# Fourier layer between attention and feed-forward: token sums first, the folded columns of X as TensorE weights

## The chip, the cores and the metric

The kernel runs on one core of a Trainium2 chip. The metric is device time in microseconds (us) from the first to the last instruction of one execution. The kernel before took 1040.67 us (median of three runs, 1038.98 to 1045.13).

## What is computed

For each of 4 batches and 8 heads, queries, keys and values are 768 x 64. Queries and keys are assigned to one of 16 centroids by cosine; a score counts only where both have the same centroid. The attention output is laid out as X (768 tokens x 512 columns) per batch, goes through a two-dimensional Fourier transform of which only the real part is kept, and through a feed-forward layer with a residual:

```python
q_assign = np.argmax(np.einsum('bhsd,hcd->bhsc', q_n, c_n), axis=-1)
k_assign = np.argmax(np.einsum('bhsd,hcd->bhsc', k_n, c_n), axis=-1)
mask = q_assign[:, :, :, None] == k_assign[:, :, None, :]
scores = np.where(mask, scale * (q @ k.T), -1e9)
x = softmax(scores) @ v                      # as batch x 768 x 512
mixed = np.real(np.fft.fft(np.fft.fft(x, axis=1), axis=2))
u = x + mixed
un = (u - mu) / np.sqrt(var + 1e-06)         # over the 512 columns
out = u + np.maximum(un @ w_ch1, 0.0) @ w_ch2
```

All is float32 outside; inside, operands are split into two fp16 parts and three products are summed.

## The kernel before

**Attention** runs in steps. A head pair has six steps, one per block of 128 queries; four pairs make a batch, 16 pairs (96 steps) the whole. A step is written here as batch.pair.block. `scores` puts 12 matmuls L320 and 4 mask matmuls L325 on PE, then DVE L339 takes a maximum, ACT L342 the exponential and L350 its high half, POOL L351 the low half, and a DMA transpose L353 lays both out as `pt`. Two steps later (three in the first 22 steps) `attend` multiplies `pt` by V (L371 to L373, 36 matmuls); at blocks 2 and 5 of a pair `finish` (L383 to L387) divides and writes X. The preparation of the next pairs (`prep`: loads L206, maxima L216 and L248, scales L48, splits L235/L236, centroid choice L263 to L293) runs in the same steps.

**Fourier layer.** When all of X of a batch is there, `fold` adds and subtracts the two token halves and the two column halves (L641, L642: DVE and POOL), splits the result into fp16 parts (`halve`, ACT L625 and DVE L626) and has each part transposed by DMA (L648). `transform` first sums over columns: three chunks of the odd part and three of the even part (matmuls L697 with 257 moving columns, L712 for a middle row), with `rest` (six PE transposes L662 to L665) for one left-over column. Each result is split again (L625, L626). Then it sums over tokens in three thirds (L697, L746, L747); each third's result is added to and subtracted from X (ACT L758, DVE L759/L760, then L764 to L767 on DVE for third 0 and POOL for the others).

**Feed-forward** works in three blocks of 256 tokens. `norm` (L802 to L817) normalizes two of X's token tiles and has them transposed by DMA (L817); `up` is 16 chunks of 12 matmuls L846 with ReLU and split (L852 to L856); `down` is 8 chunks of 12 matmuls L877, each output tile finished by L881. The feed-forward chunks of batch b are the filler of the attention steps of batch b+1; the ones of batch 3 stand alone at the end.

**What sets the order.** `Overlap.run` writes the order of PE by hand, step by step; `MIX`, `KEEP` and a credit (`fill`) choose how many filler chunks stand between `scores` and `attend` of each step. DVE, ACT, POOL and SP follow a scheduler's priorities. All Fourier, feed-forward and preparation results on PE share a pool `ps_f` of three PSUM buffers; the temporary arrays of Fourier and feed-forward share one region of on-chip memory, `arena`. SP issues every DMA, in order.

## Time and profile before

| what | value |
|---|---|
| median of three runs | 1040.67 us |
| runs | 1038.98, 1040.67, 1045.13 us |
| profiled execution, its own span | 1037.9 us |
| mean granted TensorE clock | 0.949 |
| PE busy | 919.5 us (89%) |
| DVE, ACT, POOL busy | 594.6, 604.9, 587.9 us |
| first feed-forward matmul L846 of batch 0, 1, 2, 3 | at 260.05, 489.97, 715.05, 908.75 us |

The profiled execution stands 2.8 us below the median of the timed runs. A row of the timeline gives start, duration, engine, line, operation, output and inputs, count, and in brackets the engine's idle time before it and what ended it. A row of the windows view gives, after the window and its length, the busy time of each engine with the count of instructions, the mean granted TensorE clock, the mean busy share of the DMA engines and GB/s. A PE row's duration includes the drain of its last matmul, so the pace of matmuls is read from start to start.

### The profile page before, as it was taken

What the parts mean: (1) busy time and instruction counts of PE and PEld (TensorE: products, weight loads), DVE (VectorE), ACT (ScalarE), POOL (GpSimd) and SP (SyncE); (2) the same over time, 40 slices, a digit from 0 to 9 for tenths busy, and PEclk for the clock granted to TensorE, in tenths of its full rate; (3) what the DMA queues carried; (4) which work ended last, traced back from release to release, by engine and by line L of the source; (5) the groups of instructions that cost most, each with busy time, mean ns of one, the idle gap of its engine ahead of it and who ended that gap; (6) DMA issues with size and microseconds to landing.
All of it is one profiled execution on the core that took longest, in us unless ns stands there. A gap on an engine that the chain in (4) does not pass through costs nothing.

```text
span 1037.9 us, 23603 instructions
## 1 busy us (share of the span) xinstructions
PE 919.5 (89%) x9416; PEld 592.4 (57%) x9416; DVE 594.6 (57%) x1276; ACT 604.9 (58%) x948; POOL 587.9 (57%) x694
## 2 busy tenths in 40 slices
PE   4686777667999999997999999997999999899998
...
PEclk9688878889899999998999999998999999999999
...
GB/s 264 195 256 231 281 213 192 175 144 145 157 104 179 104 148 134 124 142 189 105 144 139 138 125 152 87 149 179 114 105 131 101 119 33 82 32 41 11 12 21
DMA packets 396239, 140.01 MB, mean 135 GB/s; under 512 B 381784, under 2 KB 381792, under 8 KB 396128
## 3 DMA queue, kind: packets, MB, share of 16 engines
...
## 4 chain that ended last, share of the span: by engine, by line
PE 47%; DVE 8%; POOL 7%; DMA 7%; ACT 6%; issue 5%; SPq 0%; ACTq 0%; POOLq 0%; DVEq 0%
PE ps_f L877 19%; PE ps_f L846 17%; PE ps_big L320 4%; DMA pt<-ph 4%; POOL ph L351 3%; DMA arena<-arena 3%; DVE ps_big L339 3%; ACT ph L350 2%; PE ps_o L371 1%; PE ps_o L372 1%; PE ps_o L373 1%; ACT p L342 1%; PE ps_big L325 1%; PE ps_f L697 1%; DVE arena L626 1%
## 5 line engine op out<-in xcount | busy, mean ns | idle before, releaser
L351 POOL TENSOR_TENSOR ph<-p,ph 128x768 f16<-128x768 f32 x144 | 242.0, 1690 | 179.9 <-ACT ph L350 152.5
L846 PE MATMUL ps_f<-arena,w1h 128*128 128x256 f16 x1536 | 272.1, 277 | 24.8 <-DMA arena<-arena 15.4
L877 PE MATMUL ps_f<-w2h,arena 128*128 128x512 f16 x768 | 238.9, 379 | 0.5 <-ACT arena L855 0.5
L846 PE MATMUL ps_f<-arena,w1l 128*128 128x256 f16 x768 | 212.5, 277 | 0.0
L342 ACT ACTIVATE p<-ps_big,rmx 128x768 f32<-128x768 f32 x144 | 129.1, 900 | 128.7 <-DVE ps_big L339 119.0
L877 PEld LDWEIGHTS <-arena 128*128 128x128 f16 x1152 | 108.7, 98 | 127.2 <-issue 5.8
L846 PEld LDWEIGHTS <-w1h 128*128 128x128 f16 x1536 | 152.3, 99 | 42.3 <-issue 21.0
L856 POOL TENSOR_TENSOR arena<-arena 128x256 f16<-128x256 f32 x192 | 128.2, 678 | 74.2 <-ACT arena L855 70.9
L339 DVE TENSOR_SCALAR_CACHE_REDUCE ps_big<-ps_big,sce 128x768 f32<-128x768 f32 x144 | 141.5, 1020 | 46.7 <-PE ps_big L325 46.7
L320 PE MATMUL ps_big<-hlk,hlq 64*128 64x384 f16 x1152 | 126.2, 344 | 30.3 <-ACT p L342 17.3
L877 PE MATMUL ps_f<-w2l,arena 128*128 128x512 f16 x384 | 145.5, 379 | 0.0
L371 PE MATMUL ps_o<-v,pt 128*128 128x66 f16 x1152 | 121.4, 196 | 12.4 <-DMA pt<-p 6.4
L855 ACT ACTIVATE arena<-ps_f,wrel 128x256 f16<-128x256 f32 x192 | 90.8, 475 | 70.5 <-DVE arena L852 68.7
L852 DVE TENSOR_SCALAR arena<-ps_f,wrel 128x256 f32<-128x256 f32 x96 | 46.3, 482 | 144.6 <-POOL arena L856 82.9
L350 ACT CAST ph<-p 128x768 f16<-128x768 f32 x144 | 117.3, 831 | 15.7 <-DMA pt<-ph 15.1
L371 PEld LDWEIGHTS <-pt 128*128 128x128 f16 x1152 | 108.5, 99 | 25.7 <-issue 13.5
L372 PE MATMUL ps_o<-v,pt 128*128 128x64 f16 x1152 | 121.1, 197 | 0.0
L373 PE MATMUL ps_o<-v,pt 128*128 128x66 f16 x1152 | 120.6, 195 | 0.0
L372 PEld LDWEIGHTS <-pt 128*128 128x128 f16 x1152 | 108.9, 99 | 2.8
L373 PEld LDWEIGHTS <-pt 128*128 128x128 f16 x1152 | 109.1, 101 | 0.0
L320 PEld LDWEIGHTS <-hlq 64*128 64x128 f16 x1152 | 54.6, 98 | 90.5 <-issue 60.0
L846 PEld LDWEIGHTS <-w1l 128*128 128x128 f16 x768 | 76.1, 99 | 20.0 <-issue 10.6
...
## 6 DMA issues: line engine op xcount, KB each, us to landing
...
```

The costliest lines, as they stand in the source:

```text
L320: nc.tensor.matmul(out=ps[j][:, hf, 0:SH], lhsT=hq[rows[j], a, sl], rhs=hk[rows[j], c, hs], start=(i == 0), stop=False)
L339: self.mark = nc.vector.tensor_scalar(out=ju, in0=ps[j][:, :, 0:SH], scalar1=ne, scalar2=None, op0=ALU.mult, op1=ALU.min, accum_out=m)
L342: nc.scalar.activation(x, ju, AF.Exp, bias=m, scale=-1.0)
L350: nc.scalar.copy(out=ph[:, 0], in_=p32)
L351: nc.gpsimd.tensor_tensor(out=ph[:, 1], in0=p32, in1=ph[:, 0], op=ALU.subtract)
L371: nc.tensor.matmul(out=o[:, at:at + W], lhsT=hi, rhs=v16[:, kt, 0:W], start=(kt == 0), stop=False)
L372: nc.tensor.matmul(out=o[:, at:at + D], lhsT=hi, rhs=v16[:, kt, 66:130], start=False, stop=False)
L373: nc.tensor.matmul(out=o[:, at:at + W], lhsT=lo, rhs=v16[:, kt, 0:W], start=False, stop=(kt == ST - 1))
L846: nc.tensor.matmul(out=ps.rearrange("p (t x) -> p t x", x=P), lhsT=a[:, dc, fs], rhs=c[:, :, dc], start=(i == 0), stop=(i == 11))
L855: nc.scalar.activation(hh[:, f], ps, AF.Relu, scale=rel[:, f:f + 1])
L856: nc.gpsimd.tensor_tensor(out=hl[:, f], in0=r, in1=hh[:, f], op=ALU.subtract)
L877: nc.tensor.matmul(out=ps, lhsT=a[:, f, ts], rhs=c[:, f], start=(i == 0), stop=(i == 47))
```

## The change

Token sums come first now, and need no transposes: a folded fp16 block of X with 128 tokens on the partitions and 128 columns is itself the weight of a matmul whose moving operand is a table row of 385 (cosine) or 384 (sine) frequencies. The output has columns on the partitions, and is the weight of the second sum (over columns, 257 moving columns).

- The fold is done in four units a, b, c, d (128 x 768 elements each). Units a and b (sine and cosine) use the columns of head pairs 0 and 3, c and d those of pairs 1 and 2. The head pairs of a batch are now taken in the order 0, 3, 1, 2 (`place`), so a and b can be folded when half of the batch's pairs are done.
- `tokens` A, B, C, D are the token sums of the four units: 9 matmuls L695 each, and two L715 for the middle token in B and D. `tokens256` (R) is the sum for column 256, as two rows: 7 matmuls L729/L731. `third` then sums over columns: 14 matmuls per third of tokens (L695, L764), and 8 more in third 0 for the middle frequency.
- The DMA transposes L648 (two per batch), the PE transposes of `rest`, and 119 matmuls per batch with 257 columns go; 47 matmuls with 384 or 385 columns and 50 with 257 come.
- The generator `layer` with `MIX` gives way to plans by step: relative to the step t of a batch's last attention, `a`, `b` and the tables at t-2, `A`, `B`, `c`, `d` at t-1, `C`, `D`, `R`, third 0 and `norm` at t, thirds 1 and 2 at t+1. An `o` in a plan is one feed-forward chunk of the batch before.
- The last block's `attend` of each batch is put one step earlier, and so is the end of the batch; `norm` of block 0 is issued after third 0 instead of after the matmuls of third 1; the tables come with one set of transfers; arena offsets move.

```diff
+def place(pr):
+    b, i = divmod(pr, H // 2)
+    return b, (0, 3, 1, 2)[i]
...
 class Fourier:
-    FOLDS = ((1, ALU.subtract), (0, ALU.add))
-    FE = (0, 0, 0, 1)
+    W = (SH + 1, SH)
+    UNITS = ((0, 1), (0, 0), (1, 1), (1, 0))
+    OPS = (ALU.add, ALU.subtract)
+    FE = ((0, 0), (0, 0), (0, 0), (0, 0))
...
+    def fold(self, b, u):
...
+        e0.tensor_tensor(out=f, in0=X4[:, 0:3, qs], in1=X4[:, 3:6, qs], op=op)
...
+        e1.tensor_tensor(out=f[:, :, 0, 1:P], in0=f[:, :, 0, 1:P], in1=f[:, :, 1, P - 1:0:-1], op=op)
+        h = at(self.FH[u % 2], [P, 2, 3, P], F16)
+        self.halve(f[:, :, 0], h[:, 0], h[:, 1], s)
...
+    def tokens(self, b, u):
...
+        ps = self.psf()
+        self.three(ps[:, 0:w], [((h[:, 0, k], h[:, 1, k]), (tab[0][:, k], tab[1][:, k])) for k in range(3)], last=bool(i))
...
+        with self.tc.high_priority():
+            self.split(ps[:, 0:w], y)
...
+    def columns(self, out, i, cols):
+        tab = (self.cd, self.sd)[i]
+        ys = [self.Y[c, i] for c in range(2)]
+        self.three(out, [((y[:, 0, cols], y[:, 1, cols]), (tab[:, 0, c], tab[:, 1, c])) for c, y in enumerate(ys)],
+                   last=bool(i))
...
-    COST, KEEP, KEEP3 = 130.4, 10.5, 7.9
+    COST = 124.8
...
-    MIX = (1, 0, 0, 0, 1, 0, 0, 1, 1, 0)
-    MIX3 = (0, 0, 0, 0, 0, 0, 0, 1, 1, 1)
-    F2 = 1
+    PLAN0 = ((-2, 3.6, "Sabg"), (-1, 1.5, "AB"), (-1, 3.6, "hcd"), (0, 1.5, "CD"), (0, 3.5, "R0n"), (1, 1.5, "12"))
+    PLAN = ((-2, 3.6, "Sabg"), (-1, 1.5, "oAB"), (-1, 3.6, "hcd"), (0, 1.5, "oCD"), (0, 3.5, "oR0n"), (1, 1.5, "o12oo"))
+    PLAN3 = ((-2, 3.6, "Sabg"), (-1, 1.5, "oAB"), (-1, 3.6, "hcdooCoDoR0no12oo"),)
+    F2, F1 = 2, -2
...
-                at(t0 + st + self.LAG + (6 * pr + st < self.LATE), 3, att.attend, pr, st)
+                at(t0 + st + self.LAG + (6 * pr + st < self.LATE) - (pr % 4 == 3 and st == 5), 3, att.attend, pr, st)
...
-        ends = [T0 + 24 * (b + 1) + self.LAG for b in range(B)]
+        ends = [T0 + 24 * (b + 1) + self.LAG - 1 for b in range(B)]
...
-            at(t, 0, self.fft.fold, b)
+            for dt, order, steps in self.PLAN if 0 < b < B - 1 else (self.PLAN3 if b else self.PLAN0):
+                at(t + dt, order, self.plan, b, steps)
```

Lines of the changed kernel are 6 or more higher than those of the kernel before: L320 is L326, L339 L345, L353 L359, L387 L393, L625/L626 are L629/L630, L802 to L817 are L826 to L841, L846 is L870, L877 L901.

**PE, batch 1, from third 0 to the first feed-forward matmul.** One row for each kind of work, in the order of its first appearance. Before:

```order
L697 MATMUL ps_f<-arena 128x257
...
L371 MATMUL ps_o<-v_5322,pt 128x66
...
L48 MATMUL ps_f<-ident,amx 128x128 x3
...
L320 MATMUL ps_big<-hlk,hlq 128x384
...
L877 MATMUL ps_f<-w2h,arena 128x512
...
L846 MATMUL ps_f<-arena,w1h 128x256
```

Changed:

```order
L764 MATMUL ps_f<-arena 1x257
...
L326 MATMUL ps_big<-hlk,hlq 128x384
...
L901 MATMUL ps_f<-w2h,arena 128x512
...
L695 MATMUL ps_f<-arena 128x257
...
L269 MATMUL ps_f<-hlq,ct 32x384
...
L377 MATMUL ps_o<-v_5367,pt 128x66
...
L870 MATMUL ps_f<-arena,w1h 128x256
```

Between third 0 and the first feed-forward matmul stood three attention steps (three `scores`, three `attend`), thirds 1 and 2, the scales L48 and two `down` chunks; now there stand two `scores`, one `attend`, thirds 1 and 2, the centroid matmuls L269 and two `down` chunks. The count of score matmuls L320 ahead of the first L846 of batches 0, 1, 2 goes from 384, 684, 972 to 336, 624, 912 (L326 ahead of L870): with 12 a step, the feed-forward layers begin 4, 5 and 5 attention steps earlier in the program. For batch 3 all 1152 stand ahead of it in both.

**DVE, batch 1, from the last write of X to the end of the fold** (X_64 is X of batch 1). Before:

```order
L387 TENSOR_TENSOR X_64<-ps_o,rs 128x3x128
L248 TENSOR_REDUCE amx<-vst 128x1
L852 TENSOR_SCALAR arena<-ps_f,wrel 128x256 x2
L339 TENSOR_SCALAR ps_big,rmx<-ps_big,sce 128x2x384 x2
L201 SCALAR_TENSOR_TENSOR v_6174<-vst,scp,v_6174 128x6x64
L641 TENSOR_TENSOR arena<-X_64 128x1536
L626 SCALAR_TENSOR_TENSOR arena<-arena,vseq 128x768
```

Changed:

```order
L393 TENSOR_TENSOR X_64<-ps_o,rs 128x3x128
L664 TENSOR_TENSOR arena<-X_64 128x768
L669 TENSOR_TENSOR arena<-arena 128x3
L670 TENSOR_TENSOR arena<-arena 128x3x127
L345 TENSOR_SCALAR ps_big,rmx<-ps_big,sce 128x2x384 x2
L630 SCALAR_TENSOR_TENSOR arena<-arena,vseq 1x129
L630 SCALAR_TENSOR_TENSOR arena<-arena,vseq 128x384
```

The fold of unit c follows the last write of X at once, with half the elements of the fold before; units a and b stand some steps ahead of these rows.

**DVE and SP, batch 1, from third 0 to the norm's transposes.** DVE before, between the first update of X and the statistics of the norm:

```order
L766 TENSOR_TENSOR X_64<-X_64,arena 128x257
L404 TENSOR_TENSOR ps_f<-ps_f,floor 128x3
L405 TENSOR_SCALAR ps_f<-ps_f 128x3
L407 TENSOR_SCALAR scp<-ps_f 128x3
L408 RECIPROCAL scp<-scp 128x3
L410 TENSOR_SCALAR sce<-scp 128x1 x2
L339 TENSOR_SCALAR ps_big,rmx<-ps_big,sce 128x2x384 x2
L802 BN_STATS bst<-X_64 128x6 x2
L236 SCALAR_TENSOR_TENSOR hlq<-scr,scp,hlq 128x768
L236 SCALAR_TENSOR_TENSOR hlk<-scr,scp,hlk 128x768
L803 BN_AGGR ps_f<-bst 128x2 x2
```

Changed:

```order
L789 COPY arena<-arena 1x257
L826 BN_STATS bst<-X_64 128x6
L790 COPY arena<-arena 1x257
L792 TENSOR_TENSOR X_64<-X_64,arena 128x255
L827 BN_AGGR ps_f<-bst 128x2
L791 TENSOR_TENSOR X_64<-X_64,arena 128x257
L345 TENSOR_SCALAR ps_big,rmx<-ps_big,sce 128x2x384
L826 BN_STATS bst<-X_64 128x6
```

SP, changed:

```order
L359 DMA_TRANSPOSE pt<-ph 128x12x128
L644 DMA arena<-in_cd_dram 128x1028
L644 DMA arena<-in_sd_dram 128x1028
L359 DMA_TRANSPOSE pt<-ph 128x12x128
L841 DMA_TRANSPOSE arena<-arena 128x8x128
L907 DMA out_dram<-arena 128x512
L841 DMA_TRANSPOSE arena<-arena 128x8x128
```

On DVE the scale and split work of the next head pair (L404 to L410, L236) no longer stands between the update and the statistics. On SP the two table transfers L644, which overwrite the tables that third 2 reads, stand ahead of one `pt` transpose and of the norm's two transposes L841.

274 lines of the change are left out of this document (136 added, 138 removed).

## The prediction

> **What bounds the kernel now.** I read the page first (shares, slices, chain), then the waits of PE, then windows and timeline around the four places where a batch passes from attention to feed-forward.
>
> ```profile
> span 1037.9 us, 23603 instructions
> ...
> PE 919.5 (89%) x9416; PEld 592.4 (57%) x9416; DVE 594.6 (57%) x1276; ACT 604.9 (58%) x948; POOL 587.9 (57%) x694
> ...
> PE   4686777667999999997999999997999999899998
> ...
> PEclk9688878889899999998999999998999999999999
> ```
>
> From slice 10 on (about 260 us) PE is at 9 or more in nearly every slice: it is the bound. The slices that dip are the passages of batches 1 and 2; those under 260 us are weight preparation, attention alone and the passage of batch 0. So past 260 us time changes by PE work added or removed and by PE's waits; before it, by when the first feed-forward matmul can start.
>
> The waits of PE (engine, line, what it waited for: us in all, times, longest):
>
> ```profile
> PE ps_big L320 <- ACT p L342: 17.3, 12, 3.5
> ...
> PE ps_f L846 <- DMA arena<-arena: 15.4, 4, 5.4
> ...
> PE ps_f L697 <- DMA arena<-arena: 3.9, 4, 1.3
> ...
> PE ps_f L271 <- DVE arena L626: 2.4, 1, 2.4
> ```
>
> The 15.4 us are the first L846 of each of the four batches, waiting for the norm's transposes. The windows of the passages:
>
> ```profile
> 189.80:270.50 80.70, 56.36 (x659) 38.01 (x658) 60.57 (x126) 47.23 (x73) 52.41 (x54) 0.83 0.80 164
> 439.80:452.10 12.30, 9.84 (x102) 5.97 (x103) 7.93 (x15) 6.08 (x10) 4.71 (x4) 1.00 0.48 111
> 474.90:500.60 25.70, 20.03 (x211) 13.47 (x212) 16.36 (x43) 16.71 (x29) 22.44 (x30) 0.87 0.83 180
> 663.50:675.60 12.10, 9.87 (x102) 5.99 (x103) 7.76 (x14) 6.09 (x10) 4.65 (x4) 1.00 0.47 109
> 698.40:725.70 27.30, 20.06 (x209) 13.58 (x208) 16.46 (x43) 16.71 (x29) 22.23 (x30) 0.81 0.82 165
> 880.00:910.00 30.00, 26.05 (x180) 15.46 (x178) 16.18 (x45) 8.72 (x18) 9.12 (x17) 1.00 0.40 88
> ```
>
> In the first, PE idles 80.70 - 56.36 = 24.3 us; around the fold of batches 1 and 2 12.30 - 9.84 = 2.5 and 12.10 - 9.87 = 2.2 us; around their first L846 25.70 - 20.03 = 5.7 and 27.30 - 20.06 = 7.2 us, with the clock down to 0.87 and 0.81; at the last passage 4.0 us. Work at the lower clock costs too: (1 - 0.87) x 25.7 = 3.3 and (1 - 0.81) x 27.3 = 5.2 us of clock, partly inside the waits. I put the loss of the three later passages at 11.5, 14.6 and 4.0 us at most (idle plus clock).
>
> How long the norm takes, from the first DVE operation on third 0 to the first L846, batches 0, 1, 2, 3:
>
> ```profile
> 205.43 0.56 DVE L387 TENSOR_TENSOR X<-ps_o,rs 128x384 f32<-128x384 f32 x1
> ...
> 237.53 0.48 DVE L759 SCALAR_TENSOR_TENSOR arena<-ps_f,vseq,arena 128x257 f32<-128x257 f32 x1 [1.86 <-ACT arena L758]
> ...
> 260.05 0.37 PE L846 MATMUL ps_f<-arena,w1h 128*128 128x256 f16 x1 [4.43 <-DMA arena<-arena]
> ...
> 464.43 0.49 DVE L759 SCALAR_TENSOR_TENSOR arena<-ps_f,vseq,arena 128x257 f32<-128x257 f32 x1 [0.57 <-ACT arena L758]
> ...
> 489.97 0.37 PE L846 MATMUL ps_f<-arena,w1h 128*128 128x256 f16 x1 [3.62 <-DMA arena<-arena]
> ...
> 687.92 0.48 DVE L759 SCALAR_TENSOR_TENSOR arena<-ps_f,vseq,arena 128x257 f32<-128x257 f32 x1 [0.57 <-ACT arena L758]
> ...
> 715.05 0.37 PE L846 MATMUL ps_f<-arena,w1h 128*128 128x256 f16 x1 [5.44 <-DMA arena<-arena]
> ...
> 893.11 0.49 DVE L759 SCALAR_TENSOR_TENSOR arena<-ps_f,vseq,arena 128x257 f32<-128x257 f32 x1 [1.78 <-PE ps_f L697]
> ...
> 908.75 0.27 PE L846 MATMUL ps_f<-arena,w1h 128*128 128x256 f16 x1 [1.92 <-DMA arena<-arena]
> ```
>
> That is 22.5, 25.5, 27.1 and 15.6 us. With no attention beside it the chain takes 15.6; attention's work on DVE and ACT adds 7 to 11.5.
>
> **The change part by part.** The sum is made against 1037.9 us, the profiled execution; the median of the runs stands 2.8 us above it.
>
> *PE work of the Fourier layer.* Gone per batch are 119 matmuls of 257 columns and 6 transposes; new are 47 of 384 or 385 columns and 50 of 257.
>
> ```profile
> 461.72 1.17 PE L697 MATMUL ps_f<-arena 128*128 128x257 f16 x9
> 462.82 0.28 PE L746 MATMUL ps_f<-arena 1*128 1x257 f16 x1
> ...
> 683.86 1.15 PE L320 MATMUL ps_big<-hlk,hlq 64*128 64x384 f16 x12
> 684.94 0.34 PE L325 MATMUL ps_big<-oht 32*128 32x384 bf16 x4
> ...
> 688.91 0.20 PE L371 MATMUL ps_o<-v,pt 128*128 128x66 f16 x1
> ...
> 690.02 0.91 PE L48 MATMUL ps_f<-ident,amx 128*128 128x128 f32 x6
> ...
> 883.81 0.82 PE L697 MATMUL ps_f<-arena 128*128 128x257 f16 x6 [1.14 <-DVE arena L626]
> 884.47 0.49 PE L662 MATMUL ps_f<-ident,arena 128*1 128x128 f32 x3
> ...
> 884.92 0.26 PE L665 MATMUL ps_f<-ident,arena 1*128 1x1 f32 x2
> 886.07 0.84 PE L697 MATMUL ps_f<-arena 128*128 128x257 f16 x6 [0.90 <-DMA arena<-arena]
> ...
> 929.91 20.72 PE ps_f L877 x96
> ```
>
> From start to start, 9 matmuls of 257 columns take 1.10 us, 0.122 each; 96 of 512 take 20.72, 0.216 each. In between, 385 columns come to 0.169 by interpolation. The nearest row with 384 columns is L320, two matmuls side by side: 6 pairs in 1.08 us, 0.180 a pair. The transposes keep PE from 884.47 to 885.18, 0.7 us. Before: 119 x 0.122 + 0.7 = 15.2; after: 47 x 0.169 + 50 x 0.122 = 14.0, or 14.6 with 0.180. I take -1.2 a batch; bounds -1.6 (0.162, in proportion to the 512-column row) and +1.0 (0.216, no cheaper than 512 columns). For batch 0 it lies among idle time, so three batches count: **-3.6** (-5 to +3).
>
> *Batch 0, the earlier start.* X is complete at 205.43 + 0.56 = 206.0 in both; before, the fold then needs until 237.53 to reach third 0's update. The new pieces, by the groups of DVE and ACT (count, busy, mean ns):
>
> ```profile
> L641 DVE TENSOR_TENSOR arena<-X 128x1536 f32<-128x1536 f32 x8 | 14.1, 1757 | 1.5 <-POOL arena L856 1.3
> L626 DVE SCALAR_TENSOR_TENSOR arena<-arena,vseq 128x768 f16<-128x768 f32 x8 | 9.2, 1154 | 19.3 <-ACT arena L625 19.3
> L642 DVE TENSOR_TENSOR arena<-arena 128x765 f32<-128x765 f32 x4 | 5.1, 1285 | 0.1
> ```
>
> A unit has half of each: 0.9 + 0.6 on DVE, some 0.5 on ACT, 0.6 on DVE, about 2.6 us; with the two maxima L339 of a step between, c is ready near 209 to 211 and d near 213 to 215. A and B have run by then. C, D, R and third 0 are 20 + 7 + 22 matmuls, about 7 us of PE, with a split of some 0.9 us behind D and behind R and a `scores` between: third 0's first DVE operation at 221 to 223, against 237.53. Add a norm chain of 19.5 to 22.5 (below) and the first feed-forward matmul comes near 243 in place of 260.05: **17 earlier**. But four attention steps that ran ahead of it now run behind it. A step's `scores` from 683.86 is 1.08 + 0.27 = 1.35 us, its `attend` (688.91 to 690.02) 1.1; with the preparation matmuls among them four steps are about 11.2 us of PE, which must be done later. About 1 us of new waits goes too. Gain 17 - 11.2 - 1 = **-5** (-16, if most of the moved work falls into time that is idle anyway, to +4, if the start is only 8 earlier).
>
> *Batches 1 and 2.* Gone: the waits on L648's transposes (3.9 us over four) and on splits, and the delay of the statistics by L404 to L410 and the two splits L236, which stood between L802 and L803:
>
> ```profile
> 474.39 1.00 DVE L236 SCALAR_TENSOR_TENSOR hlq<-scr,scp,hlq 128x768 f16<-128x768 f32 x1
> ```
>
> With its twin and the five small operations that is 3 to 4 us, and the statistics no longer wait for the updates of a later third. So the chain falls from 25.5 and 27.1 to about 20 (ends: 15.6, the chain without attention, and 27). Its cover shrinks too: between third 0 and the first feed-forward matmul PE had three `scores` and three `attend` (3 x 2.45), thirds 1 and 2 (36 + 4 matmuls, 4.8), two `down` chunks (2 x 2.59) and 0.9 of L48, about 18; it now has two `scores` (2.7), one `attend` (1.1), 28 matmuls of the thirds (3.4), 8 left of third 0 (0.9), the centroid matmuls (0.5) and two `down` chunks (5.2), about 14. The wait stays: 20 - 14 = 6, less what the last `scores` waits anyway, 5.2 to 5.7. PE also waits for c and d: d is ready some 5 us after the last `attend`, with 2.5 us of idle left, as in the fold windows before. With a split of R of 0.7, 1.7 for the clock (half of a stretch of 3.4 behind the wait) and 2.1 of small waits, as `scores` has them on L342, the passages cost 2.5 + 0.7 + 5.5 + 1.7 + 2.1 = 12.5 each, against 13.1 (11.5 and 1.6 of split waits) and 14.6: **-0.6** and **-1.9** (-8 to +7 each).
>
> SP: two table transfers L644 wait for third 2's last matmul ahead of the norm's transposes. Third 2 ends some 9 us behind third 0, the transposes are issued at 15 or later, so this hides; if PE lagged by 6 us it would not. DVE's four smaller folds replace about the same work; DVE is busy 57%.
>
> On the clock, the row at 489.97 shows a 3.62 us wait, and its window stands at 0.87, while 2.5 us of idle around the fold (439.80) left it at 1.00. The Trainium skill (TensorE: Matmul & The Clock Gate, "Part 1: The HAM clock gate") says that the clock halves after an idle window of about 3.4 us and needs a busy one to return, which agrees with these windows. By it the new 2.5 us wait for d would cost no clock, and only the one at the first feed-forward matmul would, as the sum has it; were those two waits to come out under that window, the sum would be 3.4 us lower.
>
> *Batch 3.* The fourth passage has only `down` chunks as cover. Its chain of 15.6 holds one wait on third 1:
>
> ```profile
> 898.71 0.42 DVE L803 BATCH_NORM_AGGREGATE ps_f<-bst 128x2 f32<-128x6 f32 x2 [1.60 <-ACT arena L758]
> ```
>
> Without it the chain is about 13.7. The cover had three `down` chunks and thirds 1 and 2; it now has two, those thirds and 8 matmuls, 5.2 + 3.4 + 1.0 = 9.6. So the wait of 1.92 grows to about 4; R's split adds 0.7, and the norm takes a third `ps_f` buffer earlier, which holds third 1 up by an update of X's 1.4 (L758, L759, L760, 0.48 each). The gone waits of 1.14 and 0.90 at the fold stand against it: **+2** (-2 to +7).
>
> Sum: -3.6 - 5 - 0.6 - 1.9 + 2 = -9.1; 1037.9 - 9.1 + 2.8 = **1031.6 us**.
>
> **Rivals.** *The norm does not get shorter* (slower). Attention's DVE and ACT work, which holds the chain at 25.5 and 27.1 against 15.6 alone, may hold it as before: the statistics are placed earlier, but DVE, ACT and POOL carry the same work in this passage (474.90: 16.4, 16.7 and 22.4 of 25.7). Then the cover of 14 leaves 11.5 and 13 us of waiting instead of 5.5: +6 and +7.5 on the -0.6 and -1.9 above. With the chain of 15.6 kept in the last passage that is +4; batch 0 gains 4 and the PE work 3.6. Sum 5.4 + 5.6 + 4 - 4 - 3.6 = +7.4: 1048. Each us of chain costs 2, so it decides from about 24 us on, where the 9.1 are used up. For it speaks that the parts on POOL (22.4 of 25.7 busy) do not move; against it that the two operations in front of the statistics do go.
>
> *The waits vanish.* If the chain comes to 15.6 in the middle passages too and less in the last, the three later waits (3.6 + 5.4 + 1.9 = 10.9) go, and of the 8.5 us of lower clock the 5 that I put outside them. With the PE work and batch 0 as above, 10.9 + 5 + 3.6 + 5 = 24.5: 1037.9 - 24.5 + 2.8 = 1016. The row at 893.11 speaks for it, DVE's load against.
>
> *Batch 0 does not gain.* The stretch up to 270 us has DMA at 0.80 and the clock at 0.83; weight, load and `pt` transfers may hold the earlier feed-forward back, and attention's steps behind it wait as before. Then the 5 fall away, or turn to +2: 1036 to 1039. That the change would simply do nothing is this case too: its PE work differs by 3.6 us alone.
>
> **Chances.** Forecast 0.48, no gain at batch 0 0.22, norm not shorter 0.17, waits vanish 0.13. A difference under 0.5% (5.2 us) can't be told from none. Faster by more needs under 1035.5: nearly all of the first and last, a little of the second: 0.6. Slower, over 1045.9: 0.2, with what of the forecast's bounds lies there. Within: 0.2. The forecast's own bounds reach 1018 to 1045; the range takes in both rivals' ends, 1012 to 1048.
>
> **What would show it.** The first L870 at about 243 (right if before 248, wrong if after 252). In batches 1 and 2, third 0's first DVE operation to the first L870 under 22 us, and a wait there of 5 to 6; over 24 the slower rival holds. A wait of 2 to 3 us ahead of D's matmuls. L695 with 385 columns 0.16 to 0.18 apart. The clock below 1 only behind the first L870. If batch 0 is early and the end is not, the moved attention steps were dearer than 11.2 us.

## The result

The changed kernel is slower: 1079.9 us median (1075.66 to 1084.92, 4 runs) against 1040.38 us (4 runs), a ratio of 1.037 (95% interval 1.032 to 1.043). The forecast was 1031.6 us. The profiled execution took 1073.8 us, 35.9 us more than the 1037.9 us of the one before; it was the fastest of the four, and the medians lie 39.5 us apart. All step times and losses below are read from one profiled execution of each kernel. The page of the changed kernel:

```profile
span 1073.8 us, 23394 instructions
...
PE 922.1 (86%) x9284; PEld 584.1 (54%) x9304; DVE 603.8 (56%) x1316; ACT 605.8 (56%) x952; POOL 586.4 (55%) x694
...
PE   4667675678997989889989989889989999989998
...
PEclk9798888788998999999999999899999999999999
```

PE, DVE, ACT and POOL are busy about as long as before. But from slice 10 on PE shows 8 in many slices that read 9 before, and these lie between the passages from attention to feed-forward, not only in them. The waits of PE (engine, line, what it waited for: us in all, times, longest):

```profile
PE ps_f L870 <- ACT arena L879: 28.1, 16, 5.5
PE ps_big L326 <- DVE X L345: 19.4, 20, 4.3
PE ps_f L870 <- DMA arena<-arena: 19.2, 4, 8.6
PE ps_f L695 <- ACT arena L629: 10.7, 4, 6.5
PE ps_big L326 <- ACT p L348: 7.7, 8, 2.0
```

The third row is the wait for the norm's transposes that the forecast dealt with (15.4 before). The first is new in size: feed-forward matmuls that wait for the ReLU and split on ACT, inside the attention steps. How long the norm takes, from third 0's first DVE operation to the first L870, batches 0 to 3:

```profile
227.12 0.49 DVE L784 SCALAR_TENSOR_TENSOR arena<-ps_f,vseq,arena 128x257 f32<-128x257 f32 x1 [1.21 <-PE ps_f L695]
...
246.94 0.37 PE L870 MATMUL ps_f<-arena,w1h 128*128 128x256 f16 x1 [8.62 <-DMA arena<-arena]
...
463.57 0.49 DVE L784 SCALAR_TENSOR_TENSOR arena<-ps_f,vseq,arena 128x257 f32<-128x257 f32 x1 [1.22 <-PE ps_f L695]
...
482.37 0.39 PE L870 MATMUL ps_f<-arena,w1h 128*128 128x256 f16 x1 [2.99 <-DMA arena<-arena]
...
703.94 0.49 DVE L784 SCALAR_TENSOR_TENSOR arena<-ps_f,vseq,arena 128x257 f32<-128x257 f32 x1 [1.22 <-PE ps_f L695]
...
722.94 0.27 PE L870 MATMUL ps_f<-arena,w1h 128*128 128x256 f16 x1 [3.19 <-DMA arena<-arena]
...
928.40 0.49 DVE L784 SCALAR_TENSOR_TENSOR arena<-ps_f,vseq,arena 128x257 f32<-128x257 f32 x1 [1.21 <-PE ps_f L695]
...
943.31 0.37 PE L870 MATMUL ps_f<-arena,w1h 128*128 128x256 f16 x1 [4.38 <-DMA arena<-arena]
```

19.8, 18.8, 19.0 and 14.9 us, against 22.5, 25.5, 27.1 and 15.6. So the passages did get what the forecast saw in them, and batch 0 starts 13 us earlier. The time went elsewhere. From here on a step is written as pair.block, with the 16 pairs counted from 0 to 15 over the whole kernel, and not as batch.pair.block: batch 0 has pairs 0 to 3, and step 4.0 is the first of batch 1. The stretches between the passages are steps 5.2 to 8.0, 9.5 to 12.0 and 13.5 to 15.4 ("mid-way" below); the feed-forward of batches 0, 1 and 2 is the filler there. Their windows, first of the kernel before, then of the changed one:

```profile
270.50:414.60 144.10, 139.61 (x1586) 93.41 (x1587) 82.54 (x175) 88.91 (x143) 92.95 (x106) 1.00 0.69 131
517.70:637.00 119.30, 118.23 (x1305) 77.48 (x1304) 68.54 (x147) 72.99 (x114) 74.72 (x84) 1.00 0.72 134
742.80:843.90 101.10, 100.19 (x1078) 62.95 (x1077) 47.26 (x104) 57.60 (x89) 60.07 (x65) 1.00 0.60 111
```

```profile
287.00:439.80 152.80, 142.08 (x1580) 92.28 (x1579) 91.89 (x189) 88.52 (x140) 91.91 (x101) 0.97 0.71 137
545.80:676.30 130.50, 119.49 (x1349) 81.13 (x1348) 78.28 (x158) 78.16 (x127) 81.44 (x90) 0.97 0.70 138
786.80:888.30 101.50, 91.42 (x1054) 61.52 (x1053) 51.83 (x110) 60.19 (x96) 63.80 (x67) 0.97 0.67 121
```

PE's idle time (length less PE busy) was 4.5 + 1.1 + 0.9 = 6.5 us; it is 10.7 + 11.0 + 10.1 = 31.8. And the clock, 1.00 before, is 0.97 in all three: 0.03 x 384.8 = 11.5 us. Together 25.3 + 11.5 = 36.8 us that the forecast did not have. In the changed kernel all of this idle time is in waits for ACT: 12 of the 16 waits of L870 for L879 lie in these windows, 24.1 of the 28.1 us, and the 8 waits of L326 for L348, 7.7 us.

For an account of the whole, each step's length less its matmuls at the pace of undisturbed steps (`scores` 1.35, `attend` 1.11, an `up` chunk 1.31, a `down` chunk 2.59, a 257-column matmul 0.122, a 385-column one 0.17, small preparation 0.45 to 0.55 each) gives what PE lost there by waits and clock, in us:

| steps | before | changed | difference |
|---|---|---|---|
| up to 3.5 (step 4.0 begins at 189.8, now 193.9) | 90.6 | 94.7 | +4.1 |
| 4.0 to 5.1, passage of batch 0 | 36.3 | 30.2 | -6.1 |
| 5.2 to 8.0 | 6.6 | 17.4 | +10.8 |
| 8.1 to 9.4, passage of batch 1 | 14.8 | 14.3 | -0.5 |
| 9.5 to 12.0 | 2.1 | 16.4 | +14.3 |
| 12.1 to 13.4, passage of batch 2 | 16.2 | 18.7 | +2.5 |
| 13.5 to 15.4 | 2.0 | 14.0 | +12.0 |
| 15.5 to the end | 4.8 | 8.1 | +3.3 |

(In the first row 20 matmuls whose records are missing from the trace of the changed kernel are counted as work.) The sum is +40.4 us, and the matmul work by these prices is 4.5 us less: +35.9, the difference of the spans. The three mid-way rows are 10.7 before and 47.8 now, +37.1. All losses below are counted in this way.

One of these stalls, step 6.0 of the changed kernel: PE, ACT and SP.

```profile
327.07 0.37 PE L870 MATMUL ps_f<-arena,w1h 128*128 128x256 f16 x1 [4.81 <-ACT arena L879]
```

```profile
325.45 0.83 ACT L356 CAST ph<-p 128x768 f16<-128x768 f32 x1 [5.36 <-DMA pt<-ph]
```

```profile
314.02 2.64 SPq L841 DMA_TRANSPOSE arena<-arena  x2
317.32 0.38 SPq L642 DMA_DIRECT2D arena<-in_ss_dram  x1
317.75 0.48 SPq L642 DMA_DIRECT2D arena<-in_cs_dram  x1
...
320.09 0.28 SPq L644 DMA_DIRECT2D arena<-in_ny_dram  x1
320.48 4.17 SPq L359 DMA_TRANSPOSE pt<-ph  x2
```

PE waits for a ReLU (L879) that stands on ACT behind L356; L356 waits 5.36 us for a buffer that the last `pt` transfer must first have read; that transfer stands on SP behind the second norm's transposes, token tables and `ny`. Steps 10.0 and 14.0 repeat it (waits of 4.85 and 5.53). These three steps lost 6.3, 6.4 and 7.0 us; the other 28 us lie in smaller waits at 6.1, 6.2, 7.1, 7.2, 7.4, 11.1, 11.2, 15.4 and others. (L879, one of the two ReLU operations of an `up` chunk, ran on ACT right behind this L356 and L878, at 326.55.)

**Theories.** *Thin filler*: the kernel before has the Fourier layer's matmuls and leftover feed-forward spread over steps 8.1 to 9.1; the change packs the Fourier layer and eight `down` chunks into steps 8.0 to 8.2, with 12.2, 19.0 and 11.6 us of matmul work there, and step 7.5 has 12.5. The other twenty steps of a batch then have less, and where a step's matmuls are shorter than what attention's DVE, ACT, POOL and DMA need for it, PE waits. *Queue*: tables and `ny` ahead of `pt` on SP. *Maxima*: the early loads put L222 ahead of L345 on DVE at 7.1 and 11.1. *ACT order*: ReLUs behind attention's casts. *Phase*: the feed-forward's start now falls elsewhere against the head pairs, so that `up` blocks meet the second norm at a bad place.

### The profile page after: what moved, and what is told of

Same layout as the page of the kernel before. It is cut to its first block, busy times and chain, and to the rows that moved or that the text cites. A ratio compares the mean times of both kernels' runs of the same rounds, so it can differ in the third digit from the quotient of the medians.

```text
span 1073.8 us, 23394 instructions
## 1 busy us (share of the span) xinstructions
PE 922.1 (86%) x9284; PEld 584.1 (54%) x9304; DVE 603.8 (56%) x1316; ACT 605.8 (56%) x952; POOL 586.4 (55%) x694
## 4 chain that ended last, share of the span: by engine, by line
PE 36%; DVE 16%; DMA 15%; POOL 12%; ACT 11%; issue 8%; SPq 1%; ACTq 0%; POOLq 0%; DVEq 0%
PE ps_f L870 16%; PE ps_f L901 10%; DMA pt<-ph 7%; POOL ph L357 5%; PE ps_big L326 3%; ACT ph L356 3%; DVE ps_big L345 3%; ACT p L348 2%; DMA scr<-in_q_dram 2%; DMA vst<-in_v_dram 2%; DVE X L345 2%; PE ps_f L695 2%; DMA scr<-in_k_dram 2%; POOL arena L880 2%; POOL arena L840 1%
## 5 line engine op out<-in xcount | busy, mean ns | idle before, releaser
L357 POOL TENSOR_TENSOR ph<-p,ph 128x768 f16<-128x768 f32 x144 | 237.1, 1655 | 214.8 <-ACT ph L356 196.7
L870 PE MATMUL ps_f<-arena,w1h 128*128 128x256 f16 x1536 | 274.6, 278 | 47.3 <-ACT arena L879 28.1
L901 PE MATMUL ps_f<-w2h,arena 128*128 128x512 f16 x768 | 242.4, 384 | 0.0
L870 PE MATMUL ps_f<-arena,w1l 128*128 128x256 f16 x768 | 213.2, 278 | 0.0
L348 ACT ACTIVATE p<-ps_big,rmx 128x768 f32<-128x768 f32 x144 | 129.4, 900 | 114.0 <-DVE ps_big L345 99.7
L901 PEld LDWEIGHTS <-arena 128*128 128x128 f16 x1152 | 109.7, 99 | 131.1 <-issue 12.5
L880 POOL TENSOR_TENSOR arena<-arena 128x256 f16<-128x256 f32 x192 | 134.8, 711 | 83.1 <-ACT arena L879 79.0
L870 PEld LDWEIGHTS <-w1h 128*128 128x128 f16 x1536 | 152.6, 99 | 45.8 <-issue 22.4
L345 DVE TENSOR_SCALAR_CACHE_REDUCE ps_big<-ps_big,sce 128x768 f32<-128x768 f32 x144 | 141.7, 1019 | 33.2 <-PE ps_big L331 33.1
L356 ACT CAST ph<-p 128x768 f16<-128x768 f32 x144 | 118.3, 834 | 61.8 <-DMA pt<-ph 61.5
L326 PE MATMUL ps_big<-hlk,hlq 64*128 64x384 f16 x1152 | 128.6, 348 | 28.4 <-DVE X L345 19.4
L901 PE MATMUL ps_f<-w2l,arena 128*128 128x512 f16 x384 | 147.5, 384 | 0.0
L377 PE MATMUL ps_o<-v,pt 128*128 128x66 f16 x1152 | 120.3, 196 | 13.1 <-DMA pt<-p 6.9
L879 ACT ACTIVATE arena<-ps_f,wrel 128x256 f16<-128x256 f32 x192 | 91.3, 476 | 61.2 <-DVE arena L876 60.8
L377 PEld LDWEIGHTS <-pt 128*128 128x128 f16 x1152 | 107.9, 98 | 26.5 <-issue 16.4
L326 PEld LDWEIGHTS <-hlq 64*128 64x128 f16 x1152 | 55.6, 99 | 88.8 <-issue 60.2
L870 PEld LDWEIGHTS <-w1l 128*128 128x128 f16 x768 | 76.3, 99 | 39.8 <-issue 30.5
```

The lines of the kernel that those rows point to most:

```text
L326: nc.tensor.matmul(out=ps[j][:, hf, 0:SH], lhsT=hq[rows[j], a, sl], rhs=hk[rows[j], c, hs], start=(i == 0), stop=False)
L345: self.mark = nc.vector.tensor_scalar(out=ju, in0=ps[j][:, :, 0:SH], scalar1=ne, scalar2=None, op0=ALU.mult, op1=ALU.min, accum_out=m)
L348: nc.scalar.activation(x, ju, AF.Exp, bias=m, scale=-1.0)
L356: nc.scalar.copy(out=ph[:, 0], in_=p32)
L357: nc.gpsimd.tensor_tensor(out=ph[:, 1], in0=p32, in1=ph[:, 0], op=ALU.subtract)
L377: nc.tensor.matmul(out=o[:, at:at + W], lhsT=hi, rhs=v16[:, kt, 0:W], start=(kt == 0), stop=False)
```

## The experiments

Ratios are to the kernel before, run beside each, with 95% intervals. The changed kernel stands at 1.037 (1.032 to 1.043). The intervals of e1, e2, e4, e6, e8 and e13 overlap with that, so there the losses of single steps say more than the time.

### The queue in front of the transposes

**e1_no_tables**

```diff
-        for nm in ("ss", "cs"):
+        if b:      # tables' names point at a weight tile
+            ...
+        for nm in ("ss", "cs") if not b else ():
```

> The changed kernel without the token tables' transfers (L642) in batches 1 to 3: there the token sums read a piece of the weights as if it were the table, so their result is not the reference's and only the time counts. Queue theory: in steps 6.0, 10.0 and 14.0 three table transfers stand on SP behind the norm's transposes and ahead of a step's pt transposes; pt is late, ACT's cast L356 waits for a free ph in order, the feed-forward's ReLUs wait behind it on ACT, and PE has no free PSUM buffer. Then the waits of 4.8, 4.9 and 5.5 us at 327, 564 and 806 us go with the slower clock behind them, 18 to 22 us in all: about 1059 to 1062 us. Thin-filler theory: the feed-forward of a batch is spread over 4 to 5 more attention steps, each has less to cover a late chain, and the transfers are only one of many small delays: at least 3 us of each wait stay, the time falls by less than 8 us, to 1072 or more.

1073.99 us, 1.033 (1.030 to 1.036). Step 6.0 still lost 4.5 (6.3), 10.0 2.9, 14.0 4.8; the three mid-way rows sum to 36.0 in place of 47.8. Tables have a part, a quarter of the mid-way loss (11.8 us); the time fell by 6 us and not by the 18 to 22 of the queue theory.

**e4_tables_later**

```diff
+    PLAN = ((-10, 3.6, "T"), ...       # T: three of the four table transfers,
+                with self.tc.issue_after(self.att.sent.ins):   # behind a pt transfer
+                    self.fft.ahead()
```

> The changed kernel with three of the four token-table transfers of batches 1 to 3 held on SP until the pt transposes of step x.3 of the batch's third pair are issued (6.3, 10.3, 14.3), so that they no longer stand between the norm's transposes and the pt of 6.0. Queue theory, place decides: as much is saved as without the transfers, 16 to 22 us, 1058 to 1064 us. If it is the transfers' load on the DMA engines and not their place in the queue, the wait moves to steps 6.4 or 6.5 and less than 8 us are saved. Thin-filler theory: less than 8 us too, with waits of 3 us or more left at 6.0, 10.0 and 14.0.

1073.85 us, 1.032 (1.028 to 1.035). That is 6 us less, under the 8 of the thin-filler line, and steps 6.4 and 6.5 did not lose more. Steps 6.0, 10.0, 14.0 lost 4.7, 4.2 and 4.6. What still stood on SP ahead of `pt` was `ny`, which waited 2.3 us for the norm's transposes to land.

**e16_queue_clear**

```diff
-        for nm in ("ny", "cm", "sd", "cd"):
+        for nm in ("ny", "cm", "sd", "cd")[bool(b):]:
...
+        self.nc.sync.dma_start(out=at(self.NY, [1, 2], F16), in_=self.con["ny"])   # in ahead()
```

> e4_tables_later, and the tiny transfer of ny (two numbers) is held back with the tables too. In e4_tables_later it was issued on SP only after the transposes of the second norm had landed (SP waited 2.3 us for it) with the two pt transfers of step 6.0 behind it; now nothing stands between those transposes and pt but one output transfer. Computation is complete. The losses of steps 6.0, 10.0 and 14.0 were 6.3, 6.4 and 7.0 us in the changed kernel, 4.7, 4.2 and 4.6 in e4_tables_later, 0.1 in the kernel before and in e15_before_thin. If the queue ahead of pt makes them: under 2.5 each, mid-way losses of 12, 12 and 11 in place of 14.6, 14.6 and 13.8, and 1073.9 - 7 = about 1067 (1063 to 1070). If the thin step itself makes them: 4 or more each, and 1071 to 1075.

1071.76 us, 1.026 (1.022 to 1.031). SP at step 6.0 of this kernel:

```profile
314.63 2.63 SPq L848 DMA_TRANSPOSE arena<-arena  x2
317.36 0.53 SPq L914 DMA_DIRECT2D out_dram<-arena  x1
318.70 4.23 SPq L359 DMA_TRANSPOSE pt<-ph  x2
```

`pt` is issued 1.4 us behind the transposes instead of 3.8, and steps 6.0, 10.0 and 14.0 lose 2.0, 2.0 and 2.5, about what the queue theory had (under 2.5): at these three steps the queue sets the wait (19.7 became 6.5). But the mid-way rows are 14.5, 14.4 and 10.6, not 12, 12 and 11, since other thin steps lose more: 6.2 3.3 in place of 1.9, 7.2 4.3 in place of 3.2, 11.2 4.4 in place of 3.1. Of 13.2 us taken away at the three steps, 8.3 were left in the mid-way sum. The time does not decide: the median, 1071.8, lies in the other theory's range, but the kernel before took 1045.12 beside this run, and the ratio of 1.026 makes about 1068 of the 1040.38 above, which is in the queue theory's range. By the steps each theory was half right: the queue says where the stall shows, not how much is lost.

### Maxima and ACT's order

**e2_pin_max**

```diff
-    PIN, PF, PV = (), 29, 1
+    PIN, PF, PV = (1,), 29, 1      # L222 behind L345 on DVE
```

> The changed kernel with the maxima of the next pair's q and k (L222 on DVE) held behind the score maxima L345 of the step in which the program puts them, where they now stand ahead of them. DVE-order theory: the loss of 5.5 us in steps 7.1 and 7.2, and again in 11.1 and 11.2, comes from L222 waiting 4.5 us for its load ahead of L345: both go, 9 to 11 us in all, 1069 to 1071 us; the waits at 327, 564 and 806 us stay. Thin-filler theory: the late load shows in another step instead, the time stays within 4 us of 1079.9.

1076.96 us, 1.036 (1.033 to 1.038). The losses of 7.1 and 7.2 went from 5.6 to 0.4, and came back at 6.5 (0.7 to 2.8), 7.4 (1.4 to 2.6), 7.5 (0 to 1.2) and 6.0 (6.3 to 7.1). The mid-way sum is 50.0 (47.8). The stall moved.

**e5_later_and_pin** (e4 and e2 together)

> Both edits together: tables later and L222 held. If the two are separate causes the savings add, 26 to 32 us: 1048 to 1054 us. Thin-filler theory: no more than 10 us together, about 1070.

1066.17 us, 1.023 (1.020 to 1.027): mid-way 14.5, 14.0 and 7.9, together 36.4. Both reliefs together took off more (1.4%) than the two alone (0.2% and 0.5%, neither clear of the intervals), a time between the two expectations, but 26 us more than in the kernel before remain.

**e6_relu_first**

```diff
-    NT, HP = 2 * P, 0
+    NT, HP = 2 * P, 1      # ReLU and split at high priority
```

> The changed kernel with the feed-forward's ReLUs (ACT L878/L879, DVE L876) given priority over the other work that is ready on those engines. ACT-order theory: PE loses its 28.1 us of waits for L879 because the ReLUs stand behind the cast L356, which waits for a pt transpose; with the ReLUs ahead these waits fall under 10 us and 15 to 20 us are saved, 1060 to 1065. Phase theory (the second up block now lies on the steps x.5 to x.2 in which the next pair is split and loaded): the late pt then holds attend or the next scores instead, under 6 us are saved, 1074 or more.

1081.29 us, 1.039 (1.034 to 1.044). Step 6.0 lost 6.7. But the edit did not put the ReLUs ahead. ACT at step 6.0 of this kernel:

```profile
331.17 0.83 ACT L356 CAST ph<-p 128x768 f16<-128x768 f32 x1 [5.91 <-DMA pt<-ph]
331.91 0.47 ACT L878 ACTIVATE arena<-ps_f,wrel 128x256 f32<-128x256 f32 x1
332.28 0.47 ACT L879 ACTIVATE arena<-ps_f,wrel 128x256 f16<-128x256 f32 x1
```

The ReLUs still stand behind L356 and its wait for a `pt` transfer, as at 325.45 in the changed kernel, and so they do at steps 10.0 and 14.0 (waits of 5.47 and 5.55). So this run does not test the theory, and no other run does: what a ReLU ahead of L356 would be worth stays open.

### Filler per step

**e7_end32** and **e8_end26** (the steps over which a batch's feed-forward is shared out: more steps, less in each, or the reverse)

```diff
-    END = 28
+    END = 32        # e8_end26: END = 26
```

> The changed kernel with the feed-forward spread over four more steps (END 32 for 28): less filler in each step, and the second up block moves from steps 5.5 to 6.3 to steps 6.1 to 6.5, so that down chunks stand at 5.3 to 6.0. Phase theory: the losses at 6.0, 10.0 and 14.0 (6.3, 6.4 and 7.0 us over the work in the step, and 1.2, 0.4, 0.7 in the step after) fall under 2 us each; 12 to 20 us are saved, 1060 to 1068. Thin-filler theory: less filler makes every late chain show, 5 us or more are lost: 1085 or more.

> The changed kernel with the feed-forward over two steps fewer (END 26): 8% more filler in each step, and the second up block still on steps 5.5 to 6.2. Thin-filler theory: 10 us or more are saved, under 1070. Phase theory: the losses at 6.0, 10.0 and 14.0 stay at 4 us or more each and the time within 6 us of 1079.9.

e7: 1109.91 us, 1.066 (1.061 to 1.071); mid-way 33.3, 29.5 and 11.7. e8: 1069.96 us, 1.028 (1.021 to 1.035); mid-way 11.8, 10.2 and 8.5. With END 32, 28, 26 the mid-way sum is 74.5, 47.8, 30.5. In e7 the `up` block moved away from steps 6.0, 10.0 and 14.0, and these lost 1.0 to 1.1, as the phase theory had it, while 6.2 lost 8.9 and 7.5 6.2 and the time rose by 30 us: the phase says where the loss shows, and fell as a cause of its size. In e8 the block still lay on steps 5.5 to 6.2, and 6.0 lost 0.1; but with the fuller steps the second norm's transposes, the tables and `ny` went out on SP from 310.5 to 322.8, all before 6.0 began on PE (324.2), so this run does not part the filler from the queue.

**e9_before_end22** (the kernel before, its `up` block brought to steps 6.0 to 6.2, with thick filler)

```diff
-    END = 28
+    END = 22
```

> The kernel before the change, with its feed-forward over six steps fewer (END 22), which puts its second up block on steps 6.0 to 6.2, with more filler in each step than any kernel here, and leaves the passages without down chunks. Phase theory: the steps 6.0, 10.0 and 14.0, which lose nothing now (0.1 us), lose 3 us or more each, though neither Fourier layer nor tables are changed. Thin-filler theory: they stay under 1 us. In either case the passages lose their cover, 5 to 10 us in all, so the steps decide and not the total.

1091.4 us, 1.047 (1.043 to 1.051). Steps 6.0, 10.0 and 14.0 lost 0.1, mid-way 2.4, 3.0 and 0.9: no loss from that phase where filler is thick. What the mid-way steps got was missing later: the passages of batches 1 and 2 lost 32.4 and 33.8 (14.8 and 16.2), the end 27.0 (4.8), far more than the 5 to 10 us expected. Filler is a sum to be shared out; too thick in one place is too thin in the other.

**e10_spread**

```diff
-    PLAN = (..., (0, 1.5, "oCD"), (0, 3.5, "oR0n"), (1, 1.5, "o12oo"))
+    PLAN = (..., (0, 1.5, "oo"), (0, 3.5, "C"), (1, 1.5, "oD"),
+            (2, 1.5, "oR0n"), (3, 1.5, "o1"), (4, 1.5, "o2"), (5, 1.5, "o"))
-    F2 = 2, END = 28
+    F2 = (2, 6, 6, 2), END = (26.6, 25.7, 25.7, 28)
```

> The change as it is, but in batches 1 and 2 the Fourier layer and the eight down chunks behind it are spread over seven attention steps in place of three (C, D, R with third 0, third 1 and third 2 in five different steps, a chunk or two with each), so that feed-forward starts four steps later there and the later steps have more matmul work each: 8.8 us per step on the mean behind batch 1's start, against 7.8 in the changed kernel. Batch 0's steps stay at about 7.8 (its feed-forward ends 1.4 steps earlier, so a little over). Computation is complete. Theory (thin filler): what PE loses beyond its work between the passages falls from 17.4, 16.4 and 14.0 us (batches 0, 1, 2) to about 13, 6 and 6, the passages stay at about 14 to 16 each: 1079.9 - 23 = about 1057, range 1042 to 1062. Rival (the losses come from something else in the change, such as the order of the tables, the maxima or the Fourier layer's own helpers, and stay when work is spread): 1070 or more.

1067.06 us, 1.024 (1.019 to 1.029). The same three windows of this kernel:

```profile
288.30:440.10 151.80, 142.39 (x1582) 93.07 (x1583) 90.77 (x185) 89.52 (x142) 94.08 (x100) 0.97 0.71 136
542.30:675.60 133.30, 129.58 (x1411) 85.85 (x1412) 77.89 (x162) 77.72 (x126) 79.85 (x89) 1.00 0.64 135
776.40:884.60 108.20, 107.20 (x1164) 71.18 (x1165) 53.59 (x114) 61.62 (x100) 64.79 (x70) 1.00 0.63 114
```

In batches 1 and 2, where the work was spread, idle time falls from 11.0 and 10.1 to 3.7 and 1.0 and the clock is back at 1.00: losses 6.2 and 2.5. In batch 0, hardly touched, it stays at 9.4 with 0.97. The instructions are those of the changed kernel, and the second norm's transposes, three table transfers and `ny` still stand ahead of a `pt` on SP, now in steps 10.1 and 14.1, which lost 0.5 and 0.1. So the losses of these two batches go with the order of the program, in which filler is the main thing that changed; the `up` block and the second norm moved by a step or more with it, and this run does not part the two. The passages did not stay at 14 to 16, though: batch 1's lost 23.5 and batch 2's about 22, since steps 9.0 and 13.0 had no feed-forward work at all and the norm's chain stood open. That and the unchanged batch 0 are why the time is 10 us over the expectation.

**e15_before_thin** (the reverse: the kernel before, thinned)

```diff
-    END = 28
+    END = 31
```

> The kernel before, unchanged but for one number: the feed-forward chunks are shared out over more steps (END 31 in place of 28), so that each step between the passages has 7.5 to 7.7 us of matmul work in place of 8.1 to 8.3, and what is left over (4 chunks a batch, 10.4 us) is put in one place ahead of the Fourier layer. The same instructions in all, and the Fourier layer of before. Theory (thin filler): what PE loses between the passages grows from 10.7 us to 40 or more, as in the changed kernel with the same 7.5 to 7.7: 1040 + 25 to 45 = about 1072 (1060 to 1085). Rival (the loss belongs to the changed computation): the kernel before does not care, 1036 to 1046.

1062.54 us, 1.023 (1.018 to 1.028): the kernel before loses 21.6 us by this one number. Its windows:

```profile
271.10:409.40 138.30, 132.24 (x1501) 86.29 (x1501) 80.16 (x174) 84.74 (x133) 88.27 (x99) 0.99 0.72 135
526.80:642.30 115.50, 108.62 (x1210) 68.55 (x1210) 65.62 (x143) 68.68 (x107) 70.64 (x77) 1.00 0.69 134
762.40:857.90 95.50, 93.08 (x1042) 59.42 (x1041) 46.58 (x103) 59.14 (x93) 63.10 (x67) 1.00 0.65 117
```

Idle time is 6.1 + 6.9 + 2.4 = 15.4 us (6.5). The rival (the kernel before does not care) fell; but the mid-way losses are 10.0, 8.7 and 4.2, 22.9 together and not 40 or more, and another 9 us lie in the passages of batches 1 and 2 (19.9 and 20.0). So this thinning explains 12 of the 37.1 us. But it did not go as far as the change. Without the steps that take leftover chunks (7.5, 8.0, 11.5 and 12.0), a mid-way step has on the mean, in the three stretches, 8.07, 8.41 and 8.25 us of matmul work in the kernel before, 7.64, 7.76 and 7.60 here, and 7.37, 7.44 and 7.29 in the changed kernel: two thirds of the way, and not "the same 7.5 to 7.7". e8_end26 is the nearer match from the other side: with 7.90, 7.88 and 7.73 us a step its mid-way loss is 30.5, more than the 22.9 here with less work a step. So the changed kernel loses more at like filler.

### The folds of batch 0

DVE ahead of step 4.0 in the changed kernel (4.0 begins at 193.88, when the first of the two L345 at 192.81 and 193.75 is done):

```profile
186.09 0.98 DVE L664 TENSOR_TENSOR arena<-X 128x768 f32<-128x768 f32 x1
186.99 1.00 DVE L345 TENSOR_SCALAR_CACHE_REDUCE X<-ps_big,sce 128x768 f32<-128x768 f32 x1
...
188.94 0.54 DVE L670 TENSOR_TENSOR arena<-arena 128x381 f32<-128x381 f32 x1
191.24 1.64 DVE L630 SCALAR_TENSOR_TENSOR arena<-arena,vseq 128x384 f16<-128x384 f32 x1 [1.76 <-ACT arena L629]
192.81 1.00 DVE L345 TENSOR_SCALAR_CACHE_REDUCE X<-ps_big,sce 128x768 f32<-128x768 f32 x1
```

Before the third of these maxima (the second, at 187.93, is not shown) DVE stands idle for 1.76 us, waiting for a high half on ACT, and then makes the low half first, in order.

**e12_spread_fold_late**

```diff
-    PLAN0 = ((-2, 3.6, "Sabg"), (-1, 1.5, "AB"), (-1, 3.6, "hcd"), (0, 1.5, "CD"), ...
+    PLAN0 = ((-2, 3.6, "Sg"), (-1, 3.6, "habcd"), (0, 1.5, "ABCD"), ...
```

> e10_spread, but in batch 0 the folds of the first half of X come together with those of the second half, behind the last attend, and A and B behind them. So it tells what folding early is worth in the first passage. If the early folds cost attention's start what the trace of the changed kernel suggests (step 4.0 begins 4.1 us later there, with folds a and b between score maxima), that comes back: step 4.0 begins near 190; the fold then takes longer behind the last attend, two more units of about 2.6 us and A and B with 18 matmuls (3 us), so the first feed-forward matmul comes some 4 to 8 us later than in e10_spread. Sum about 0 (-3 to +4). If the later start of step 4.0 has another cause, e10_spread's gain at the passage is lost alone: +4 to +8.

1071.11 us, 1.029 (1.023 to 1.035), against 1067.06 for e10_spread. In this kernel A and B read the folds of c and d, which had taken the place of a's and b's, so its output differs; its instructions are as many. It did not test what it was made for: with high priority the scheduler left a and b on DVE where they had been, and only A and B came later. Step 4.0 began at 195.2, the first feed-forward matmul at 251.84 instead of 248.12. So it says only that A and B ahead of the last `attend` are worth about 3.7 us there.

**e13_fold_behind** (on the changed kernel)

```diff
+    PLAN0 = ((-2, 3.6, "Sg"), (-1, 1.5, "ab"), (-1, 3.6, "ABhcd"), ...
+            elif b == 0 and c in "ab":
+                with self.tc.issue_after(self.att.mark.ins):   # behind L345 of step 4.0
+                    self.fft.step(b, c)
```

> The change as it is, but in batch 0 the folds a and b are issued on DVE behind the score maxima of step 4.0, so none stands between the maxima of steps 3.4, 3.5 and 4.0, and A and B run behind that step's attend. Computation is complete. In the kernel before, step 4.0 begins at 189.8 us; in the changed kernel at 193.9, in e12_spread_fold_late, where the folds kept their place on DVE, at 195.2. If the folds between the maxima are what delays the start: 4.0 begins at 190 (189 to 191.5), the first feed-forward matmul comes at about 243 to 245 in place of 246.9, and the time is 1079.9 - 3 = about 1077 (1074 to 1079). If not: 4.0 begins at 193 or later and the time is 1080 or more.

1077.65 us, 1.036 (1.032 to 1.040). Its DVE:

```profile
184.95 1.01 DVE L345 TENSOR_SCALAR_CACHE_REDUCE X<-ps_big,sce 128x768 f32<-128x768 f32 x1
...
188.50 1.02 DVE L345 TENSOR_SCALAR_CACHE_REDUCE X<-ps_big,sce 128x768 f32<-128x768 f32 x1 [1.60 <-PE ps_big L331]
```

The maxima wait for PE again, as in the kernel before, and step 4.0 begins at 190.2 in place of 193.9: the folds between the maxima cause that delay. The loss up to 3.5 is 90.9 (94.7; 90.6 in the kernel before). But A and B now wait for their folds: the passage loses 35.0 in place of 30.2, and the first feed-forward matmul comes at 246.77, as in the changed kernel (246.94), not at 243 to 245. The time is as expected, but not by the expected way, and no different from the changed kernel's by their intervals.

### Together

**e11_spread_tables** (e10_spread and e4_tables_later)

> e10_spread with three of the four transfers of token tables held back on the SP queue to ten steps ahead of the next passage, as in e4_tables_later. Thin filler: with fuller steps there is room for the pt transfer to wait its turn, so 0 to 3 us below e10_spread. If the queue has a part of its own that cover does not hide: 6 us below, as between the changed kernel and e4_tables_later (6.1).

1061.35 us, 1.019 (1.014 to 1.024), 5.7 below e10_spread: the size that the second line of the expectation had, but not its reason. Most of it is in batch 0's thin steps (mid-way 11.5 in place of 16.4; 6.0 1.2 in place of 6.0); in the thick batches 1 and 2 the mid-way loss hardly changes (6.3 and 1.6 in place of 6.2 and 2.5). Here a late queue cost only where filler is thin.

**e14_all** (e11_spread_tables with e13's folds, and one `down` chunk moved from 8.1 to 9.0)

```diff
-    (0, 1.5, "oo")
+    (0, 1.5, "o")
```

> e11_spread_tables with the folds of e13_fold_behind, and with one down chunk of batches 1 and 2 moved from step 8.1 (12.1), where PE lost 0.0 us, to 9.0 (13.0), which had no feed-forward work at all and lost 3 to 4 us, so that 9.0 covers more of the norm's chain. Computation is complete. By thin filler, step 9.0's loss goes (2 to 4 us each, and as much of the 8 us wait behind it as the chunk covers, 2.6): about -8; by the folds -3: 1061.4 - 11 = about 1050 (1045 to 1056). If the chain of the norm sets the end whatever covers it: 1058 or more.

1053.53 us, 1.012 (1.008 to 1.016). Step 9.0 lost 0.1 in place of 3.0, 13.0 1.2 in place of 3.5; behind it 13.1 lost 5.2 in place of 8.1, but 9.1 7.8 in place of 7.4, and steps 8.1 and 12.1, which gave the chunk up, 2.1 and 2.0 in place of 0.0. So the passage of batch 2 lost some 4 us less and that of batch 1 no less than in e11_spread_tables. The mid-way rows are 11.7, 5.9 and 2.3, the passages 33.6, 22.1 and 18.2, the end 8.2.

**e17_all_clear** (e14_all with `ny` held back)

> e14_all with ny held back as well. Its steps 10.0 and 14.0 already lose only 0.1 and step 6.0 0.7, so both theories expect little: 0 to 3 us below e14_all, 1050 to 1054. A larger gain would mean that ny's place on SP costs elsewhere too.

1056.17 us, 1.012 (1.008 to 1.015), with 1045.12 for the kernel before beside it (1040.9 beside e14_all). By the ratios there is no gain, as both theories had it for thick steps.

No version beat the kernel before.

## Why the prediction was wrong, by its own steps

**PE's pace was right.** Rows of the changed kernel:

```profile
434.07 3.10 PE L695 MATMUL ps_f<-arena 128*128 128x384 f16 x18
437.11 0.49 PE L715 MATMUL ps_f<-arena 1*128 1x384 f16 x2
```

18 matmuls of 384 and 385 columns in 3.04 us, 0.169 each, as interpolated.

**The passages were nearly right, in part by luck.** The first L870 came at 246.94 ("about 243, right if before 248"), 13.1 us earlier and not 17: third 0's first DVE operation came at 227.12 and not at 221 to 223, in part because step 4.0 began 4.1 us later, while the norm's chain of 19.8 lay in the forecast's 19.5 to 22.5. Less the 11.2 us of the moved steps that leaves 1.9 us of gain, and the first two rows of the table say the same, +4.1 - 6.1 = -2.0, against a forecast of -5. In batches 1 and 2 the chain is 18.8 and 19.0 (forecast 20), so the slower rival, a norm that does not get shorter, did not happen, although the time came out beyond its 1048. The wait at the first L870 is 2.99 and 3.19, smaller than the 5 to 6 forecast. The losses there are -0.5 and +2.5 (forecast -0.6 and -1.9), at the end +3.3 (+2): a wait of 4.38 where about 4 was forecast. That batch 1 came out so near is luck: its wait at the first L870 is 2 to 3 us smaller, and step 8.1, with the wait for D, lost 5.6 (12.1: 9.5) where the sum had 2.5 and 0.7 for the split of R.

**The step that failed** is the first: "So past 260 us time changes by PE work added or removed and by PE's waits". It is true, but the sum then took PE's waits at the four passages only and let the stretches between keep their 9s. The four attention steps that batch 0's earlier start moved behind the first feed-forward matmul were priced at their matmuls, 11.2 us; the five of batches 1 and 2 each, and the packing of Fourier layer and `down` chunks into three steps, at nothing. All of this takes filler away from the other steps: 8.07, 8.41 and 8.25 us of matmul work in a mid-way step became 7.37, 7.44 and 7.29. The term that stood in the sum with 0 is +37.1 us. The text had named the sign of it: "If batch 0 is early and the end is not, the moved attention steps were dearer than 11.2 us."

What the runs show of this term: the filler per step moves it in both kernels (74.5, 47.8 and 30.5 with three values of END; 16.4 and 14.0 down to 6.2 and 2.5 by spreading alone; 10.7 up to 22.9 by thinning the kernel before); and at steps 6.0, 10.0 and 14.0 the transfers ahead of `pt` set the wait (19.7 to 6.5 without them), of which 8.3 us stay gained mid-way. What stays open is how the 37.1 us divide. Thinned two thirds as far, the kernel before loses 12. Queue and maxima together took 11.4 off the changed kernel (e5_later_and_pin); if that adds to the 12, some 13 are left. The last third of the thinning probably has a part in them, but its size was not measured, and no single cause of the rest was found. And PE's idle time between the passages is all in waits for ACT (24.1 and 7.7 us), mostly for ReLUs behind attention's L356 and L348, while no run changed that order; so the ACT theory stands untested beside thin filler.

**The folds a and b** were costed through their own 2.6 us and DVE's 57%: an average, while at 186 to 193 us the score maxima that PE waited for stood behind them in DVE's order. They delay step 4.0 by 3.7 us (e13_fold_behind); moving them gives little back, since A and B then come later.

**The wait for D** was put at 2 to 3 us with no cost in clock. It is 1.25 + 1.55 in batch 1 and 1.69 + 2.81 in batch 2, and the clock falls: see below. "The clock below 1 only behind the first L870" was wrong. Behind that L870 itself the sum had 1.7 us of clock each: in batch 1 the window 482.40 to 486.00 stands at 0.54, which is 1.7; in batch 2 the one from 722.90 to 727.00 stands at 1.00.

**What the spread shows of the rest.** With filler spread, the tables later and the folds behind (e14_all) the losses are still 21.4 us above the kernel before, against 4.5 us of work saved: the passage of batch 1 (+7.3), batch 0's mid-way steps (+5.1), batch 1's (+3.8) and the end (+3.4) are the largest parts. The saving of matmul work, forecast as 1.2 us a batch, comes out as 4.5 in all when the matmuls are counted at the prices above; it is small beside what the order costs here, and PE's busy time did not fall (919.5 and 922.1).
